# Second-stage tokens in the weight landing buffers, and two output-weight loads in flight

## The chip, the cores and the metric

The kernel runs on one core of a Trainium2 chip. What counts is the device time of one execution, in microseconds: the median over the runs of a kernel. Beside it stands one profiled execution, with the span from its first to its last instruction and a trace of every engine. The engines are TensorE (PE), VectorE (DVE), ScalarE (ACT), GpSimd (POOL) and SyncE (SP). In this kernel SP issues all the transfers between memory and the core's own memory (SBUF), one after the other, from one queue.

## The reference

Block-causal attention over 4 batches of 8 heads (576 tokens, 64 wide), then a first feed-forward block with three input matrices, then a second one with a gate. All values are float32.

```python
scores = np.where(mask, scale * np.matmul(q, k.transpose(0, 1, 3, 2)), -1e9)
attn = softmax(scores)                                # block 64, causal
x = heads_merged(np.matmul(attn, v))                  # 2304 x 512
h = np.maximum(np.maximum(x @ w1, x @ w2), x @ w3)    # 768 wide
x = h @ w_out                                         # moe: 2304 x 512
gate = 1.0 / (1.0 + np.exp(-(x @ w_gate)))            # 1536 wide
out = gate * (x @ w_val) @ w_out                      # moe2: 2304 x 512
```

## The kernel before, in words

Every float32 operand is split into a rounded high part and the rest (`fp32r`), and each product is three matmuls: high by high, high by low, low by high (L535 to L537, L574 to L576, L1220 to L1222).

**First stage** (attention and the first block), TensorE 0 to 475.5 us. Attention heads come in pairs (`job`), the first block in token groups (`gates`, `outs`): groups 0 to 3 are the early 256 tokens of each batch, 4 to 7 the late 320. A gate block of a group is three groups of twelve matmuls (`experts`) into two PSUM banks `ps_m`; ACT copies the first result to `m`, DVE takes two maxima (`larger`, L545), ACT and DVE split the maximum into `HR` (`high_h`, L558, and `low_h`). Six blocks are followed by four column blocks of the projection (`project`), whose results leave through `x2s` (L97 or L93) to `x2d` in memory (`store`, L595, three stores for each column block of a late group). The last group, 7, has its six gate blocks from 433.2 to about 465 and its projection until 475.5. While the first stage runs, the second stage's weights are also *parked*: each 64-bit weight piece is loaded (`take`, `praw`), shifted (L759), prepared on ACT (L755) and joined to float32 words (L770), and stored to memory again. `park_pair` does this for 24 pieces of the gate and value weights, and writes the seven combinations (`pairs`) that a seven-product block multiplication needs; `park_out` does it for the 12 pieces of the output weights (`outw` to `outs`). All of it uses the pool `raw` of four buffers of 4 KB: a piece takes one for its load and one for its joined words.

The order of each engine in the first stage comes from a planner in the kernel (`plan`). An `Op` has an engine, a cost, what it depends on, and for parking an earliest time: piece n of the pairs stands at `park0 + park * n`, piece f of the output weights `parko * f` after the last pair. The list `order_` holds what the next load has to wait for. The planned order is written out as it stands, and each engine then works it off in sequence.

**Second stage**, TensorE from 475.5 us. Tokens come in three chunks of 768. `take_x` loads a chunk (`xraw`, 1.5 MB), forms four differences with DVE (`t`, pool `tt`, L1116) and splits four blocks and the three kept combinations into `xc0` to `xc6` (ACT L1120 and DVE L102): eighteen instructions. `after_group` only keeps each of them behind a given conversion of group 7 on its engine. `take_w` loads parts x, z, y of an expert's weights (`wr`, four buffers), splits them on ACT (L1159) and on DVE or POOL (L102), and stores the low part for later chunks (`lowp`, L1166). TensorE runs seven products of six matmuls for each of the twelve experts: for the first one the products 0, 5, 4, 1, 6, then for each further one 0, 5, 4, 3 of the expert before, 1, 2 of the expert before, 6. Then the output projection of the chunk follows. DVE, ACT, POOL and SP are ordered here by a scheduler from the written times.

The second stage's pools are allocated one after the other from the bottom of SBUF, over the first stage's closed ones. Which first-stage tile lies under a second-stage tile decides what its first writer waits for. From the bottom, the first stage has `XT` (the attention's output, 26 KB, read by the gate matmuls), the four `raw` buffers, `tmp` (the `m`), `x2s`, eight weight tiles `w`, `HR`, and then the attention's own tiles. In the kernel before, `xr`, `ost`, `hid0` and the first bytes of `wr` lie on `XT`, the rest of `wr` and the first `pt` on `raw`, and `tt` on the end of `HR`.

Of the kernel before, what the change touches and what calls it, by code (L numbers as in the profile page):

```python
# [61 lines left out]
    "load": 14.95,  # L62
    "park0": 112,
    "park": 18.3,
    "parko": 8.0,
    "slack": 100.0,
    "spare": 0.17,
    "start": 53.02,
# [10 lines left out]
def block_attention_moe_moe(ctx: ExitStack, tc, kq1, v1, kq2, vt, wa, wb, out):  # L79
# [5 lines left out]
    def f32(ap):  # L85
        return ap.bitcast(F32)
# [38 lines left out]
    def load(out, src):  # L125
        nc.sync.dma_start(out=out.bitcast(U64) if wide else f32(out), in_=src)
# [39 lines left out]
    def act(n, acc=0):  # L166
        return ("A", 0.19 + 0.00073 * n + 0.2 * acc)
# [481 lines left out]
    t, vn = P["t0"], 0  # L649

    def visit(t):
        for j, s in visits[vn]:
            place[j.i, s] = t
            t += LEN[s][int(j.late)]
        return t

    while vn <= ends[0]:
        t = visit(t) + P["gap0"]
# [12 lines left out]
    for k, (mm, upto) in enumerate(stretches):  # L671
        n_v = ends[upto] + 1 - vn if upto < 2 * B else 0
        v0 = vn
        for n, (i, f, w) in enumerate(mm):
# [4 lines left out]
            while vn < v0 + n_v and (vn - v0 + 1) * (len(mm) - P["tail" if k > 3 else "tail1"] * (k > 0)) <= (n + 1) * n_v:  # L679
                t = visit(t)  # L680
# [3 lines left out]
    def build():  # L684
# [57 lines left out]
        def word_ops(i, t, ring, dest, dring=None):  # L742
            box = {}

            def take():
                box["x"] = raw_p.tile([128, PC * (1 + wide)], U32, tag="raw", name="praw")
                load(box["x"], wb[i])

            def words():
                w = box["x"].rearrange("p (n w) -> p n w", w=2)  # L750
                return w[:, :, 0], w[:, :, 1], w[:, :, 1].bitcast(F32)

            def first_part():
                x = words()[2]
                A.activation(x, x, AF.Prelu, scale=2.0 ** -112, alpha=2.0 ** 32)  # L755

            def shift():
                lo = words()[0]
                V.tensor_scalar(out=lo, in0=lo, scalar1=29, scalar2=None, op0=ALU.logical_shift_right)  # L759

            def two(x):
                return x.rearrange("p (a n) -> p a n", a=2)

            def join():
                o = dest()
                if not wide:
                    V.tensor_copy(o, two(f32(box["x"])))
                    return
                lo, hi, _ = words()
                V.scalar_tensor_tensor(  # L770
                    out=o.bitcast(U32), in0=two(hi), scalar=3, in1=two(lo),
                    op0=ALU.logical_shift_left, op1=ALU.bitwise_or,
                )

            ld = Op("S", 0.1, take, ring, ring="raw", size=512e3)
            new, deps = [ld], [ld]
            if wide:
                p = Op(*act(PC), first_part, [ld])
                s = Op("V", 0.36, shift, [ld])
                deps = [p, s]  # L780
                new += deps
            j = Op("V", 0.72, join, deps, ring=dring)
            new.append(j)
            for o in new:
                o.early, o.late = t, t + P["slack"]
            ld.early = t - P["load"]
            ld.frees = [j]
            return ld, j

        def put(out, src, deps, t):  # L790
            d = Op("S", 0.1, lambda: nc.sync.dma_start(out=out, in_=src()), deps, size=512e3)
            d.early, d.late = t, t + P["slack"]
            return d

        order_ = []
# [47 lines left out]
        def park_out(f):  # L843
            t = P["park0"] + P["park"] * NF2 + P["parko"] * f
            box = {}

            def dest():
                box["d"] = raw_p.tile([128, PC], F32, tag="raw", name="outw")
                return box["d"].rearrange("p (a n) -> p a n", a=2)

            ld, j = word_ops(3 * f + 2, t, list(order_), dest, "raw")
            order_[:] = [j]
            j.frees = [put(outs_d[f], lambda: box["d"], [j], t)]

        never = Op("V", 0.0, lambda: None, [])
# [206 lines left out]
    def pool(name, bufs, **kw):  # L1062
        return ctx.enter_context(tc.tile_pool(name=name, bufs=bufs, reuse_waits="tile", **kw))
# [4 lines left out]
    def hidden(n):  # L1068
        p = pool(f"hid{len(HID)}", 1)
        HID.extend(p.tile([128, 2, HC], F32R, name=f"hid{len(HID) + k}") for k in range(n))  # L1070
# [3 lines left out]
    def combos(ks):  # L1074
        p = pool(f"xc{len(XC)}", 1)
        for k in ks:
            XC[k] = p.tile([128, 2, 2, N2], F32R, name=f"xc{k}")

    xr_p = pool("xr", 1)
    ost_p = pool("ost", 3)  # L1080
    hidden(1)
    wr_p = pool("wr", 4)
    pt_p = pool("pt", 17)
    wg_p = pool("wg", 2)
    ow_p = pool("ow", 4)
    hidden(11)
    tt_p = pool("tt", 2)
    combos((0, 4, 5, 1, 6, 3, 2))
    warm = pool("warm", 1).tile([128, 8], F32, name="warm")
    acc_p = pool("acc", 8, space=PSUM)  # L1090
    PD, OU = 6 * 0.1735, 3 * 0.2317
# [195 lines left out]
    t = TB  # L1287
# [10 lines left out]
    for c in range(TOK // HC):  # L1298
# [11 lines left out]
        def second(n, t):  # L1310
            on(t, product(c, n, 1, "a", False))
            t += PD
            finish(c, n, 0, 0, None, t + 0.01)
            return t
# [27 lines left out]
        for n in range(NF2):  # L1342
            t = first(n, t)
            if n:
                t = fourth(n - 1, t)
            t = second(n, t)
            if n:
                t = third(n - 1, t)
            t = seventh(n, t)
            if 6 <= n < 10:  # L1350
                take_o(c, n - 6, t + 1.5)
        for f in range(NF2):
            for i in range(6):
                if f == 0 and i == 3:
                    t = third(NF2 - 1, fourth(NF2 - 1, t))
# [70 lines left out]
```

## Time and profile before

| what | us |
|---|---|
| median of 3 runs | 903.88 (903.22 to 905.01) |
| profiled execution, its own time | 905.0 |
| its span, first to last instruction | 903.1 |
| TensorE busy | 874.9 (97%), mean granted clock 0.992 |
| DVE, ACT, POOL busy | 587.3, 447.0, 97.2 |
| chain that ended last | PE 91%, DMA 4%, DVE 3%, SP's queue 1% |

The page divides the span into 40 slices of 22.6 us. TensorE's busy share is 9 tenths or more in nearly all; lower are the first two, one in the middle of the span, and the last. The page's list of groups gives for each line and engine the busy time, the mean duration of one instruction, and the idle time ahead of it with what ended it. The granted clock is shown as a share of the full 2.4 GHz. In a timeline row the first number is the start, the second the duration, and the bracket the idle time of that engine just before the instruction and what released it.

### The profile page before, as it was taken

How to read it: one execution, taken by the hardware profiler on the slowest of the kernel's cores; microseconds unless marked ns; L12 is line 12 of the kernel's file. 1: busy time of each engine (PE TensorE's matmuls, PEld its weight loads, DVE VectorE, ACT ScalarE, POOL GpSimd, SP SyncE). 2: the span in 40 equal slices, each digit the busy share in tenths (PEclk: the TensorE clock that was granted, in tenths of full speed). 3: DMA queues.
4: the chain of work that ended last, by engine and by line, in shares of the span. 5: the costliest groups of instructions: out<-in, count | busy, mean ns of one | idle time of the engine just before them, and what ended most of it. 6: DMA issues, size and time to landing. Idle time of an engine off the chain costs nothing.

```text
span 903.1 us, 15107 instructions
## 1 busy us (share of the span) xinstructions
PE 874.9 (97%) x5432; PEld 794.6 (88%) x5432; DVE 587.3 (65%) x1367; ACT 447.0 (49%) x1014; POOL 97.2 (11%) x91
## 2 busy tenths in 40 slices
PE   5899999999999999999996999999999999999997
PEld 4788889887989898899995999988999988999986
DVE  7999859996789699685338788731555621555400
ACT  7897547562554364353224555622666622666311
POOL 0000000000000000000003444300232300222300
PEclk9999999999999999999997999999999999999999
DMA  9921244445534534423446779854789853788232
GB/s 341 371 82 36 86 166 146 145 138 184 180 102 150 185 103 140 131 76 120 155 171 212 267 242 310 313 158 135 249 257 307 302 150 123 246 261 298 87 105 81
DMA packets 82810, 165.09 MB, mean 183 GB/s; under 512 B 10800, under 2 KB 23600, under 8 KB 82736
## 3 DMA queue, kind: packets, MB, share of 16 engines
q1 hardware_dynamic: 82736, 164.14, 54.8%
q8 instruction: 42, 0.69, 0.3%
q14 instruction: 32, 0.26, 0.1%
HBM read 126.35 MB, written 37.75 MB: 182 GB/s over the span
## 4 chain that ended last, share of the span: by engine, by line
PE 91%; DMA 4%; DVE 3%; SPq 1%; issue 0%; ACT 0%; DVEq 0%; ACTq 0%
PE acc L1220 10%; PE acc L1222 10%; PE acc L1221 10%; PE ps_m L535 8%; PE ps_m L537 8%; PE ps_m L536 8%; PE acc L1276 5%; PE acc L1275 5%; PE acc L1274 5%; PE ps_o L488 5%; PE ps_t L452 4%; PE ps_s L376 3%; PE ps_m L574 2%; PE ps_m L576 2%; PE ps_m L575 2%; DMA qk<-in_kq_dram 2%
## 5 line engine op out<-in xcount | busy, mean ns | idle before, releaser
L535 PE MATMUL ps_m<-XT,w 128*128 128x320 f32 (+2 forms) x504 | 163.7, 325 | 2.7 <-DVE x2s L97 2.7
L537 PE MATMUL ps_m<-XT,w 128*128 128x320 f32 (+2 forms) x504 | 158.0, 313 | 0.2 <-DVE w L102 0.2
L536 PE MATMUL ps_m<-XT,w 128*128 128x320 f32 (+2 forms) x504 | 157.9, 313 | 0.0
L535 PEld LDWEIGHTS ps_m<-XT,w 128*128 128x128 f32 x504 | 95.1, 189 | 10.5 <-issue 3.5
L537 PEld LDWEIGHTS ps_m<-XT,w 128*128 128x128 f32 x504 | 95.0, 188 | 3.4 <-DVE w L102 0.5
L536 PEld LDWEIGHTS ps_m<-XT,w 128*128 128x128 f32 x504 | 95.2, 189 | 2.7 <-DVE XT L102 0.2
L400 ACT ACTIVATE E<-ps_s,nm 128x256 f32<-128x256 f32 (+3 forms) x128 | 66.3, 526 | 40.5 <-PE ps_t L452 33.1
L1275 PE MATMUL acc<-ow,hid 128*128 128x512 f32 x216 | 84.2, 390 | 0.0
L1276 PE MATMUL acc<-ow,hid 128*128 128x512 f32 x216 | 84.2, 390 | 0.0
L1274 PE MATMUL acc<-ow,hid 128*128 128x512 f32 x216 | 84.1, 389 | 0.0
L1220 PE MATMUL acc<-xc,wgx 128*128 128x384 f32 x216 | 73.5, 340 | 3.5 <-ACT xc L1120 3.5
L1222 PE MATMUL acc<-xc,wgx 128*128 128x384 f32 x216 | 73.1, 338 | 1.3 <-POOL wgx L102 1.3
L1221 PE MATMUL acc<-xc,wgx 128*128 128x384 f32 x216 | 73.2, 339 | 0.8 <-DVE xc L102 0.8
L97 DVE COPY osb<-acc 128x512 f32<-128x512 f32 x6 | 4.2, 692 | 95.5 <-PE acc L1276 88.5
L545 DVE TENSOR_TENSOR m<-ps_m,m 128x320 f32<-128x320 f32 (+2 forms) x84 | 41.7, 496 | 29.0 <-PE ps_m L537 28.4
L1188 ACT CAST ow<-or 128x512 fp32r<-128x512 f32 x36 | 22.3, 621 | 73.4 <-PE acc L1276 55.4
L1233 DVE TENSOR_TENSOR u<-acc,p 128x384 f32<-128x384 f32 x72 | 39.9, 554 | 26.6 <-PE acc L1222 19.6
L395 DVE TENSOR_REDUCE nm<-ps_s 128x1 f32<-128x256 f32 (+3 forms) x128 | 55.0, 472 | 2.2 <-ACT E L400 2.2
L102 POOL TENSOR_TENSOR wgx<-wr,wgx 128x768 fp32r<-128x768 f32 x1 | 1.8, 1810 | 474.2 <-DMA x2d<-x2s 474.2
L1233 DVE TENSOR_TENSOR u<-acc,u 128x384 f32<-128x384 f32 x72 | 40.1, 557 | 18.1 <-PE acc L1222 16.8
L452 PE MATMUL ps_t<-ident,E 128*128 128x128 f32 x320 | 44.9, 278 | 6.2 <-DVE E L99 4.3
L1220 PE MATMUL acc<-xc,wgz 128*128 128x384 f32 x144 | 48.8, 339 | 1.9 <-DVE u L1233 1.1
(122 smaller groups left out, 2092.9 us busy)
## 6 DMA issues: line engine op xcount, KB each, us to landing
praw<-in_wb_dram SPq DMA_DIRECT2D x36, 512.0 KB, 4.3
wr<-pairs SPq DMA_DIRECT2D x72, 256.0 KB, 3.5
wr<-pairs SPq DMA_DIRECT2D x36, 384.0 KB, 4.3
or<-outs SPq DMA_DIRECT2D x36, 256.0 KB, 3.7
wgx<-lowp SPq DMA_DIRECT2D x24, 384.0 KB, 3.7
wland<-in_wa_dram SPq DMA_DIRECT2D x5, 1536.0 KB, 16.1
qk<-in_kq_dram SPq DMA_DIRECT2D x16, 480.0 KB, 3.4
wgz<-lowp SPq DMA_DIRECT2D x24, 256.0 KB, 4.2
```

The lines of the kernel that those rows point to most:

```text
L400: A.activation(E[h][:, e : e + 128 * (t + 1)], j.s[h, t], AF.Exp, bias=j.nm[:, c : c + 1], scale=1.0, accum_out=j.sm[:, c : c + 1],)
L452: T.transpose(ps[:, 128 * i : 128 * i + 128], E[h][:, e : e + 128], ident)
L535: T.matmul(ps, wt[:, 0, w, k], xh[:, k], start=(k == 0), stop=False)
L536: T.matmul(ps, wt[:, 0, w, k], xl[:, k], start=False, stop=False)
L537: T.matmul(ps, wt[:, 1, w, k], xh[:, k], start=False, stop=(k == KD - 1))
L1220: T.matmul(ps, w[:, 0, h], x[:, 0, h], start=start and h == 0, stop=False, skip_group_check=True)
L1221: T.matmul(ps, w[:, 0, h], x[:, 1, h], start=False, stop=False, skip_group_check=True)
L1222: T.matmul(ps, w[:, 1, h], x[:, 0, h], start=False, stop=h == 1, skip_group_check=True)
L1233: V.tensor_tensor(out=o, in0=BK[c, n, b][:, :N2], in1=x, op=ALU.add)
L1274: T.matmul(ps, h[:, 0, ct], w[:, 0], start=(f == 0), stop=False)
L1275: T.matmul(ps, h[:, 0, ct], w[:, 1], start=False, stop=False)
L1276: T.matmul(ps, h[:, 1, ct], w[:, 0], start=False, stop=(f == NF2 - 1))
```

## The change

Two things are changed. The parking of output weights is planned every 4 us instead of every 8, and a load waits for the piece two before it (`order_[:1]` of a list of two) instead of the piece before it. And the second stage's pools are allocated in another order: `wr` and two `hid` tiles come to lie on `XT`, `ost` on the first `raw` buffer, `xr` exactly on the other three, the `pt` tiles on `tmp`, `x2s` and the first weight tiles, `xc6` on a weight tile, and `tt` with the remaining `xc` tiles on the attention's memory behind `HR`. No instruction is added or removed.

```diff
-    "parko": 8.0,
+    "parko": 4.0,
...
-            ld, j = word_ops(3 * f + 2, t, list(order_), dest, "raw")
-            order_[:] = [j]
+            ld, j = word_ops(3 * f + 2, t, order_[:1], dest, "raw")
+            order_[:] = order_[-1:] + [j]
...
+    wr_p = pool("wr", 4)
+    hidden(2)
+    ost_p = pool("ost", 3)
     xr_p = pool("xr", 1)
-    ost_p = pool("ost", 3)
-    hidden(1)
-    wr_p = pool("wr", 4)
     pt_p = pool("pt", 17)
     wg_p = pool("wg", 2)
+    combos((6,))
     ow_p = pool("ow", 4)
-    hidden(11)
+    hidden(10)
     tt_p = pool("tt", 2)
-    combos((0, 4, 5, 1, 6, 3, 2))
+    combos((0, 4, 5, 1, 3, 2))
```

TensorE's order stays as it was. On SP, before, the end of the parking, the load of the tokens and the first weight loads follow one another (`praw` a parking load, `outs` a parking store, `wr` the weights' raw parts):

```order
L791 DMA outs_95<-outw 128x512
L126 DMA praw<-in_wb_dram 128x512
L791 DMA outs_96<-outw 128x512
L1106 DMA xraw<-x2d 128x4x768
L1155 DMA wr<-pairs_73 128x768
L1155 DMA wr<-pairs_73 128x512 x2
```

After the change, right behind the last parking store, SP has this (the first three stores are the first column block of group 6's projection):

```order
L595 DMA x2d<-x2s 128x128
L595 DMA x2d<-x2s 128x64
L595 DMA x2d<-x2s 128x128
L1107 DMA xraw<-x2d 128x4x768
L595 DMA x2d<-x2s 128x128
L595 DMA x2d<-x2s 128x64
L595 DMA x2d<-x2s 128x128 x2
L595 DMA x2d<-x2s 128x64
L595 DMA x2d<-x2s 128x128 x2
L595 DMA x2d<-x2s 128x64
L595 DMA x2d<-x2s 128x128
L1156 DMA wr<-pairs_73 128x768
```

The token load has moved ahead of the rest of group 6's stores, and so ahead of all of group 7's gate blocks. On DVE, before, two gate blocks of group 7 (`m` the maxima, `HR` the low part) have parking work between them:

```order
L545 TENSOR_TENSOR m_5556<-ps_m,m_5536 128x320
L545 TENSOR_TENSOR m_5571<-ps_m,m_5556 128x320
L102 TENSOR_TENSOR HR<-m_5571,HR 128x320
L759 TENSOR_SCALAR praw<-praw 128x512
L770 SCALAR_TENSOR_TENSOR outw<-praw 128x512
L545 TENSOR_TENSOR m_5607<-ps_m,m_5588 128x320
L545 TENSOR_TENSOR m_5625<-ps_m,m_5607 128x320
```

After the change the same place has the tokens' differences and low parts (`t` a difference, `xc_5926` to `xc_5928` low parts of token blocks):

```order
L102 TENSOR_TENSOR HR<-m_5590,HR 128x320
L102 TENSOR_TENSOR xc_5926<-t_5943,xc_5926 128x768
L1117 TENSOR_TENSOR t_5955<-xraw,t_5943 128x768
L545 TENSOR_TENSOR m_5622<-ps_m,m_5607 128x320
L545 TENSOR_TENSOR m_5637<-ps_m,m_5622 128x320
L102 TENSOR_TENSOR HR<-m_5637,HR 128x320
L102 TENSOR_TENSOR xc_5927<-t_5955,xc_5927 128x768
L102 TENSOR_TENSOR xc_5928<-xraw,xc_5928 128x768
L1117 TENSOR_TENSOR t_5969<-xraw,t_5955 128x768
L545 TENSOR_TENSOR m_5669<-ps_m,m_5654 128x320
```

Of the eighteen token instructions only the two of `xc6` still stand behind group 7 on their engines. In the attention, on DVE before, one parked piece stands between a softmax's scaling (`E_151`) and the split of the attention's output (`XT`), at 380.7 us of the trace:

```order
L545 TENSOR_TENSOR m_4854<-ps_m,m_4837 128x320
L99 TENSOR_SCALAR E_151<-E_151,rc 128x512
L759 TENSOR_SCALAR praw<-praw 128x512
L770 SCALAR_TENSOR_TENSOR outw<-praw 128x512
L97 CAST XT<-ps_o 128x320
L102 TENSOR_TENSOR XT<-ps_o,XT 128x320
```

After the change there are two, and the high part of `XT` is ACT's:

```order
L545 TENSOR_TENSOR m_4863<-ps_m,m_4846 128x320
L99 TENSOR_SCALAR E_151<-E_151,rc 128x512
L759 TENSOR_SCALAR praw<-praw 128x512 x2
L770 SCALAR_TENSOR_TENSOR outw<-praw 128x512 x2
L102 TENSOR_TENSOR XT<-ps_o,XT 128x320
```

The other pieces of the second half have moved in the same way, to between 381 and 425 us of the trace, the last of them ahead of the first `x2s` copy of group 6.

## Rows read from the trace of the kernel before

**Rows 1.** TensorE's waits, 475 to 496 us: us in total, times, longest.
```profile
PE acc L1220 <- ACT xc L1120: 3.5, 1, 3.5
PE acc L1222 <- POOL wgx L102: 1.3, 1, 1.3
PE acc L1220 <- DVE u L1233: 1.1, 1, 1.1
PE acc L1220 <- ACT p L1304: 0.8, 1, 0.8
PE acc L1221 <- DVE xc L102: 0.8, 1, 0.8
```

**Rows 2.** Windows: length; PE, PEld, DVE, ACT, POOL busy; clock, DMA, GB/s.
```profile
475.50:495.98 20.48, 12.95 (x49) 11.27 (x49) 17.25 (x18) 9.14 (x15) 7.05 (x4) 0.75 0.66 201
495.98:516.46 20.48, 20.48 (x120) 20.48 (x120) 15.97 (x25) 12.28 (x23) 9.21 (x8) 1.00 0.81 273
```

**Rows 3.** SP's queue around the border, timeline: start, us, what.
```profile
460.88 0.32 SPq L791 DMA_DIRECT2D outs<-outw  x1
465.04 0.54 SPq L1106 DMA_DIRECT2D xraw<-x2d  x1
...
482.86 4.11 SPq L595 DMA_DIRECT2D x2d<-x2s  x5
```

**Rows 4.** DMA issues (pairs' parking; its end; the border): KB, median us to landing.
```profile
praw<-in_wb_dram SPq DMA_DIRECT2D x23, 512.0 KB, 4.7
...
praw<-in_wb_dram SPq DMA_DIRECT2D x5, 512.0 KB, 3.5
outs<-outw SPq DMA_DIRECT2D x6, 256.0 KB, 2.1
...
xraw<-x2d SPq DMA_DIRECT2D x1, 1536.0 KB, 7.3
```

**Rows 5.** Timeline of DVE and POOL at the border.
```profile
475.60 2.57 DVE L1116 TENSOR_TENSOR t<-xraw 128x768 f32<-128x768 f32 x1 [0.41 <-PE ps_m L576]
...
485.60 0.94 DVE L1116 TENSOR_TENSOR t<-xraw 128x768 f32<-128x768 f32 x1
...
475.55 1.81 POOL L102 TENSOR_TENSOR wgx<-wr,wgx 128x768 fp32r<-128x768 f32 x1 [474.24 <-DMA x2d<-x2s]
```

**Rows 6.** Timeline of DVE, then ACT, 365 to 436 us.
```profile
369.22 0.43 DVE L759 TENSOR_SCALAR praw<-praw 128x512 uint32<-128x512 uint32 x1 [5.02 <-DMA praw<-in_wb_dram]
...
400.81 0.49 DVE L545 TENSOR_TENSOR m<-ps_m,m 128x320 f32<-128x320 f32 x1 [1.09 <-PE ps_m L537]
...
411.10 0.49 DVE L97 CAST XT<-ps_o 128x320 fp32r<-128x320 f32 x1 [1.24 <-PE ps_o L488]
...
425.44 0.49 DVE L97 COPY x2s<-ps_m 128x320 f32<-128x320 f32 x1 [1.80 <-PE ps_m L576]
...
435.12 0.43 ACT L543 COPY m<-ps_m 128x320 f32<-128x320 f32 x1 [0.87 <-PE ps_m L537]
```

**Rows 7.** Timeline of DVE, first maximum of a late gate block of group 7.
```profile
458.07 0.49 DVE L545 TENSOR_TENSOR m<-ps_m,m 128x320 f32<-128x320 f32 x1 [2.08 <-PE ps_m L537]
```

**Rows 8.** Tile `wr`, 460 to 540 us: ns min/median/max; last, us to landing.
```profile
L1159 ACT CAST wgx<-wr x9: 826/836/838, 474.6 to 532.6; 128x768 fp32r<-128x768 f32 x9
L1159 ACT CAST wgz<-wr x9: 604/616/622, 475.4 to 537.1; 128x512 fp32r<-128x512 f32 x9
L102 POOL TENSOR_TENSOR wgz<-wr,wgz x9: 1292/1609/2005, 477.3 to 538.6; 128x512 fp32r<-128x512 f32 x9
...
L102 DVE TENSOR_TENSOR wgx<-wr,wgx x8: 946/958/1144, 487.3 to 533.5; 128x768 fp32r<-128x768 f32 x8
...
DMA to landing us min/median/max: 2.7/4.1/8.8
```

**Rows 9.** Window in the attention, columns as in rows 2.
```profile
380.00:390.00 10.00, 10.00 (x82) 8.84 (x79) 9.59 (x27) 3.75 (x10) 0.00 (x0) 1.00 0.37 113
```

**Rows 10.** TensorE's waits, 330 to 476 us: us in total, times, longest.
```profile
PE ps_m L535 <- DVE x2s L97: 1.7, 1, 1.7
```

## Prediction, made before the change was run

> **What bounds the kernel now.** I read the page first: TensorE is busy for 97% of the span and makes up 91% of the chain that ended last, so only a moment in which it stands still, or runs at its lower clock, can be won. The windows along the span then show where it stands: at the head, at the tail, and at the border between the two stages. The list of its waits in that border stretch [rows 1] has five entries, 3.5 + 1.3 + 1.1 + 0.8 + 0.8 = 7.5 us, and all five name work on the second stage's first tokens or first weights. The two windows of equal length [rows 2] say what the border costs in all: 475.50 to 495.98 holds 48 of the second stage's matmuls (the 49th of the row is the first stage's last, in flight at the edge), the next 20.48 us hold 118 starts (the row counts 120, two of them cut by the edges). So one matmul needs 20.48/118 = 0.1735 us, 48 need 8.3 us, and the border wastes 20.48 - 8.33 = **12.15 us**: 7.5 us of waits, and 4.6 us because after the gaps the granted clock is 0.75 on the mean (part of it at the 1.2 GHz level) and the array refills.
>
> Next I asked why the tokens are late. The queue on SP [rows 3] stores the last parked output weight at 460.88 and issues the load of `xraw` only at 465.04: its place in memory is that of `XT`, which the last gate matmul reads until then. The load takes 7.3 us [rows 4], and DVE starts the first difference `t` at 475.60 [rows 5], released by the last projection matmul, as `tt` lies on `HR`. Everything behind it, eighteen conversions on two engines, runs while TensorE waits.
>
> **The change part by part.** *The tokens' place.* `xraw` now covers three of the four `raw` buffers, whose last user is the parking, and `tt` lies in the attention's memory, free since about 425. In the new order of SP the load stands behind the stores of the last-but-one projection's first column block, that is at 425.44 [rows 6] plus the copy and three stores: about 427.3, instead of 465.04. It took 7.3 us with four weight loads queued behind it, so it lands by 434.6. Nothing is added; the eighteen conversions move.
>
> *Where they move to.* In the new order of DVE two or three of them stand between the `HR` subtraction of one gate block and the first maximum of the next. In the trace DVE is idle there for 2.08 us in the blocks without parking work [rows 7], and parking work is gone from all of them. Two pieces of 0.94 us (the quiet `t` row [rows 5]) make 1.9 us, which fits; three make 2.8 us, 0.8 too many, and the second maximum has room of about 1.2 us to take it up. So I cost them at nothing; if that cover were gone, 0.8 us twice. The duration is a choice: the same instruction took 2.57 us at 475.60 and 0.94 at 485.60 [rows 5], and the first ran while GpSimd worked (its row starts at 475.55). I take 0.94, since GpSimd has no instruction before the border in the new order either. The Trainium skill, page "SBUF — State Buffer", section "Who interferes with whom", says a VectorE instruction with two SBUF inputs is held off entirely by a GpSimd instruction that reads SBUF; the trace agrees (2.57 against 0.94). By it alone the sum stays: the moved pieces would leave GpSimd's company.
>
> *What is left at the border.* The four `wr` buffers now lie in `XT`, so the first weight loads are issued at 465.04, no longer behind 1.5 MB of tokens. With the median landing of 4.1 us the first is in at 469.1, ACT casts 0.84 us, GpSimd's longest conversion takes 2.0 us [rows 8]: 472, before TensorE comes at 475.5. With the worst landing, 8.8, it is 476.7, about 1 us late. Of the tokens only `xc6` is left: DVE runs the last `x2s` copy (0.49 [rows 6]), `wgy` (two thirds of a `wgx`, some 0.7), `xc6` and `wgx` (0.95 each [rows 5, 8]), 3.1 us from 475.6, then `u` (384 columns where a maximum of 320 takes 0.49 [rows 7], so some 0.6) to 479.3. TensorE's fifth product, which needs it, would start at 475.5 + 4 x 1.04 = 479.7. So the first five products run through.
>
> *The second pair of weights* loses its lead, and here I see a price. Part z of the second expert is loaded after the last three token stores: 476.1 + 3 x 0.82 (five took 4.11 [rows 3]) = 478.6 at the worst, 0.4 for the store ahead, so issued by 479.0; 4.1 to land, 0.62 on ACT, 1.3 to 2.0 on GpSimd [rows 8]: 485.0 to 485.7. TensorE wants it after nine products and two matmuls, 475.5 + 9 x 1.04 + 0.35 = 485.2. Part x of the third is issued 2 us later, 481.0, lands at 485.1, 1.8 us for both conversions: 486.9, some queueing on ACT, wanted at 475.5 + 12 x 1.04 + 0.35 = 488.3. Bounds: no stall with the quickest landing (2.7), some 3.5 us with the slowest (8.8). I take **0.5 us**, near the median. After that each load is a whole expert (7.3 us) ahead, as in the trace, and TensorE is full until the tail.
>
> *The parking.* Twelve pieces, each a load of 512 KB, a shift (0.43 [rows 6]) and a join on DVE and a store: none is added, but all twelve now end before 425.44 instead of 460.88, so five or six more of them, some 1.1 us of DVE each by the 512 columns, meet the attention, where DVE is busy 9.59 of 10 us [rows 9] in the worst stretch. The new order puts one more pair there at 381 and takes a copy of 0.49 to ACT in exchange (+0.6), one at 400 and one at 409, where DVE was idle for 1.09 and 1.24 us [rows 6]. From 330 to 476 TensorE waits for another engine once [rows 10], so the lag of a few tenths has to use up a lead first. The first piece keeps what it has: DVE stood until 369.22 for its load [rows 6], with an `x2s` copy behind it, and that copy is the one wait, 1.7 us, of [rows 10]. Bounds: a gain of that 1.7 if the load comes sooner, a loss of 5.5 us (five pieces in full) if nothing hides them. I take **0.3 us** lost, nearest to the rows with idle time. Two loads in flight landed in 4.7 us while pairs were parked, one alone in 3.5 [rows 4]; with 4.7 the pieces that the new order has at 412 and 415.5 come 0.5 to 1 us late, beside the 1.24 us of idle DVE. The Trainium skill, page "DMA: Bandwidth & Descriptors", section "Issuing engines are not separate DMA queues", says all transfers run on the same 16 engines and interleave; by it the second load buys start-up time only, not bandwidth, and that speaks for the 4.7. The sum would not move.
>
> *ACT's new wait.* The warm-up of the sigmoid now stands ahead of the last stretch's first `m` copy and waits for `xraw` (434.6). That copy ran at 435.12 [rows 6], and TensorE needs its bank a gate group (twelve matmuls of 320 columns, 1.7 us) later: hidden, unless the load lands after 436.5.
>
> **The sum**, against the profiled execution (905.0 us, span 903.1, so 1.9 around it): -12.15 + 0.5 + 0.3 = -11.35, 893.7. That execution lies 1.1 above the median of the three runs, 903.88, so the forecast for the median is **892.5 us**.
>
> **The rivals.** *Weights come late* (the border's wait is replaced by another): landing took up to 8.8 us [rows 8]; then z and x of the next experts stall TensorE by 3 to 4 us, and half-clock matmuls after the gap add up to 2: 895.5 to 898.5. For it: the lead of the second pair is near nothing. Against: few bytes move at 476 to 481.
> *Parking crowds the attention*: DVE lags at 381 to 425 and a few evictions or transposes come late, 1 to 4 us: 893.5 to 896.5. Against it is the idle time at 400 to 425.
> *Slower than before*: the `raw` ring has four buffers and each piece takes two, one for the load and one for the joined words. If the second load must wait until the store before has landed, a piece takes 3.5 to 4.7 + 1.1 + 0.4 + 2.1 = 7.1 to 8.3 us [rows 4]; twelve from 364.5 end at 450 or later, while DVE's order puts the last one ahead of the `x2s` copy of 425.44 [rows 6]. TensorE would stand some 25 us: about 917. It decides from 1.4 us of delay for each of the last eight pieces (11.35/8). Against: in the new order each load waits for a store at least two stores back.
> *It does not do what it says*: `xraw` still lands near the border because the parking drags, without holding TensorE: 903.9. Against it stands its row in SP's order.
>
> **How the numbers follow.** Forecast 0.70 (890.5 to 894.2), late weights 0.13, crowding 0.10, no change 0.03, slower 0.04. The range 890.0 to 897.5 takes in the forecast with its bounds, crowding, and the lower half of late weights, and leaves out about 0.15. A measurement of this kernel tells about 0.2% from no change: faster 0.93, within 0.03, slower 0.04.
>
> **What would show it.** `xraw` issued near 427 and landed near 434; DVE's `t` rows between 440 and 462, at about 0.95 us; TensorE's second-stage matmuls 0.17 us apart from 475.6 on, no granted clock under 1.0 there; the next 20 us free of waits over 1 us. Wrong would be: a TensorE wait on `wgz` or `wgx` of several us at 485 to 490, a wait on DVE or ACT between 371 and 437, or loads of `praw` issued only after the store just before them has landed.

## The result, and the profile after

The changed kernel takes **895.9 us** (median; 895.0 to 896.7) against 903.56 us for the kernel before beside it: a ratio of 0.9912, 95% interval 0.9895 to 0.9929. Three more comparisons, told of below, gave 0.9899, 0.9911 and 0.9895, that is 894.5, 896.3 and 894.5 us. So the change gains 7.7 to 9.7 us, about 1%. The forecast was 892.5 with a range of 890.0 to 897.5: the direction is right and the time lies in the range, but the gain was put 1.7 to 3.7 us too high. This part is about where these went.

First the border. These are the same two windows as [rows 2], then the list of TensorE's waits that answers to [rows 10], of the kernel after. Columns of the first: window; its length; PE, PEld, DVE, ACT, POOL busy with their instructions; granted clock, DMA share, GB/s.

```profile
475.50:495.98 20.48, 20.48 (x120) 20.48 (x120) 12.95 (x22) 9.98 (x19) 6.56 (x5) 1.00 0.87 288
495.98:516.46 20.48, 20.11 (x115) 19.47 (x114) 15.87 (x26) 11.82 (x24) 10.59 (x9) 1.00 0.89 295
```

```profile
PE ps_m L535 <- DVE x2s L97: 1.8, 1, 1.8
```

In the first window TensorE was busy for 12.95 us and now is for all 20.48, with 120 matmuls where there were 49, and the granted clock is 1.00 (the 2.4 GHz level) where it was 0.75 on the mean. The list of waits between 475 and 496 us that held the five entries of [rows 1] is empty. The second window has turned the other way: 20.48 us busy before, 20.11 now, and the DMA share stands at 0.89.

SP's queue and DVE's timeline show why the border is clean (start, length, engine, line, operation, tiles; in brackets the idle time before it):

```profile
427.76 0.54 SPq L1107 DMA_DIRECT2D xraw<-x2d  x1
...
465.40 1.74 SPq L1156 DMA_DIRECT2D wr<-pairs  x4
```

```profile
440.43 0.95 DVE L1117 TENSOR_TENSOR t<-xraw 128x768 f32<-128x768 f32 x1
...
446.58 0.95 DVE L1117 TENSOR_TENSOR t<-xraw,t 128x768 f32<-128x768 f32 x1
...
452.73 0.95 DVE L1117 TENSOR_TENSOR t<-xraw,t 128x768 f32<-128x768 f32 x1
453.60 0.48 DVE L545 TENSOR_TENSOR m<-ps_m,m 128x320 f32<-128x320 f32 x1
454.84 0.49 DVE L545 TENSOR_TENSOR m<-ps_m,m 128x320 f32<-128x320 f32 x1 [0.76 <-PE ps_m L537]
```

The load of `xraw` is issued at 427.8 and not at 465.04 [rows 3], lands in 7.3 us, and the differences are made from 440 on, between the gate blocks, at 0.95 us each. Where three pieces stand in a row (450.99 to 453.60) the first maximum is some 0.45 us late (by the blocks' step of 5.28 us it would stand at 453.15), and the idle time ahead of the second falls to 0.76 from 1.20; TensorE does not wait.

Both traces hold the same 5432 matmuls in the same order, so their starts can be set side by side one by one. Four stretches come out (the last projection matmul is the 3272nd; us; the four columns on the right are profiles of the changed kernel, the last three from the experiments):

| stretch | before | after | again | beside | third |
|---|---|---|---|---|---|
| start to the last projection matmul | 475.3 | 475.6 | 475.2 | 475.4 | 476.1 |
| from there over 49 starts (the border) | 20.73 | 8.47 | 8.47 | 8.47 | 8.47 |
| the next 430 (nearly all the rest of the first chunk's pairs) | 75.77 | 77.55 | 76.75 | 80.21 | 78.15 |
| the last 1681 | 326.25 | 326.25 | 326.25 | 326.25 | 326.25 |

The border gives 12.26 us against the one profile of the kernel before, in every profile of the changed kernel. The stretch behind it costs 1.0 to 4.4 us more than before, 2.4 on the mean, and another amount in each execution. These are TensorE's waits there (484 to 600 us), of the first profile, then of the one called "beside":

```profile
PE acc L1221 <- DVE u L1234: 1.7, 3, 1.2
```

```profile
PE acc L1221 <- ACT wgz L1160: 1.8, 1, 1.8
PE acc L1221 <- DVE u L1234: 1.7, 3, 1.2
PE acc L1223 <- DVE wgx L102: 0.2, 1, 0.2
```

All the entries on `u` are one kind: the fourth product of an expert (its weights are `wgy`) needs a PSUM bank that DVE's addition `u` must have read. The longest of them, at 545.20, is not new: the same matmul waits 0.9 us for `u` in the kernel before, at 555.33.

### The profile page after: what moved, and what is told of

Its sections match the earlier page's. It is cut to its first block, busy times and chain, and to the rows that moved or that the text cites. A ratio compares the mean times of both kernels' runs of the same rounds, so it can differ in the third digit from the quotient of the medians.

```text
span 892.9 us, 15107 instructions
## 1 busy us (share of the span) xinstructions
PE 870.0 (97%) x5432; PEld 789.6 (88%) x5432; DVE 582.0 (65%) x1367; ACT 446.0 (50%) x1014; POOL 96.4 (11%) x91
## 4 chain that ended last, share of the span: by engine, by line
PE 85%; DMA 7%; DVE 3%; SPq 2%; issue 1%; ACT 1%; POOL 1%; ACTq 0%; POOLq 0%; DVEq 0%
PE ps_m L535 9%; PE ps_m L537 8%; PE ps_m L536 8%; PE acc L1221 7%; PE acc L1222 7%; PE acc L1223 7%; PE acc L1276 5%; PE acc L1277 5%; PE acc L1275 5%; PE ps_o L488 5%; PE ps_t L452 4%; PE ps_s L376 3%; PE ps_m L574 2%; PE ps_m L576 2%; PE ps_m L575 2%; DMA qk<-in_kq_dram 2%
## 5 line engine op out<-in xcount | busy, mean ns | idle before, releaser
L1223 PE MATMUL acc<-xc,wgx 128*128 128x384 f32 x216 | 72.2, 334 | 0.0
L1221 PE MATMUL acc<-xc,wgx 128*128 128x384 f32 x216 | 72.2, 334 | 0.0
L1222 PE MATMUL acc<-xc,wgx 128*128 128x384 f32 x216 | 72.2, 334 | 0.0
L1221 PE MATMUL acc<-xc,wgy 128*128 128x384 f32 x144 | 48.6, 337 | 1.8 <-DVE u L1234 1.7
```

What stands on the lines that cost most here:

```text
L1221: T.matmul(ps, w[:, 0, h], x[:, 0, h], start=start and h == 0, stop=False, skip_group_check=True)
L1222: T.matmul(ps, w[:, 0, h], x[:, 1, h], start=False, stop=False, skip_group_check=True)
L1223: T.matmul(ps, w[:, 1, h], x[:, 0, h], start=False, stop=h == 1, skip_group_check=True)
```

## The experiments

**The same kernel again.**

> The changed kernel a second time, so that the size of its gain does not hang on two profiled executions. By medians it gained 7.7 us (895.9 against 903.56), by the two profiled executions 10.1, while matmul for matmul the border alone gave 12.1. Theory (border 12.1 gained, about 1.7 given back in the first chunk by VectorE's late u additions, the rest is which execution was profiled): 894.5 to 896.5 beside a median of before of 903 to 904, and in the profile the four late products again, 1 to 2.5 us in all. Rival (something that varies between executions takes 2 us at the border or in the attention): the profile of this run shows the border's gain under 11 us, or TensorE waits before 475 us of over 1 us that the first profile did not have.

Measured: 894.53 us against 903.78, ratio 0.9899 (0.9885 to 0.9912). The border is 8.47 us to the hundredth, and TensorE waits for `u` twice, 1.4 us in all. The theory holds; between these two profiles the part before 475 us differs by less than half a microsecond.

**The places in memory alone.** The new pools, and the parking as before, one load in flight:

```diff
-    "parko": 4.0,
+    "parko": 8.0,
...
-            ld, j = word_ops(3 * f + 2, t, order_[:1], dest, "raw")
-            order_[:] = order_[-1:] + [j]
+            ld, j = word_ops(3 * f + 2, t, list(order_), dest, "raw")
+            order_[:] = [j]
```

> The new places in memory alone; the parking keeps one load in flight. The raw buffers that xraw now lies on are then free only when the last parked store, issued at 460.9, has landed: xraw issued at about 463, landed at 470, instead of 434. Theory (the parking is what brings the tokens early, and the tokens' conversions are the border): the first t starts at 470 to 471, thirteen pieces of VectorE at 0.5 to 0.95 us end near 484, the fifth product, wanted at 479.7, waits some 4 us, and the clock falls with it: 897 to 900, half of the gain. Rival (the new places do it all, the parking is not needed): 895 to 896.5, no TensorE wait over 1 us between 475 and 496. Rival (VectorE, waiting for the tokens, holds back the last projection copies, which stand behind t in its order): TensorE waits on x2s before 476 and 900 or more.

Measured: 902.15 us, ratio 0.9988 (0.9977 to 0.9999). The border takes 18.0 us, a gain of 2.7 where the whole change gains 12.3. The first theory forecast half of the gain and a wait at the fifth product; it failed. The third possibility is what happened, a little later than it said. TensorE's waits of this kernel from 475 to 500 us, then DVE's timeline:

```profile
PE acc L1221 <- DVE x2s L97: 6.9, 1, 6.9
```

```profile
466.87 0.96 DVE L1117 TENSOR_TENSOR t<-xraw 128x768 f32<-128x768 f32 x1
...
473.75 2.57 DVE L1117 TENSOR_TENSOR t<-xraw,t 128x768 f32<-128x768 f32 x1
476.24 2.02 DVE L102 TENSOR_TENSOR xc<-xraw,xc 128x768 fp32r<-128x768 f32 x1
478.19 0.94 DVE L1117 TENSOR_TENSOR t<-xraw 128x768 f32<-128x768 f32 x1
479.06 0.68 DVE L102 TENSOR_TENSOR wgy<-wr,wgy 128x512 fp32r<-128x512 f32 x1
479.66 0.95 DVE L102 TENSOR_TENSOR xc<-t,xc 128x768 fp32r<-128x768 f32 x1
480.52 0.48 DVE L97 COPY x2s<-ps_m 128x320 f32<-128x320 f32 x1
```

The tokens are in at 466.9, since `xraw` is issued at 460.05, right behind the last parked store. Behind the copy at 469.00, ten pieces (nine of the tokens and a `wgy`) stand ahead of the next copy `x2s` of the last projection, which runs at 480.52. The second stage's first product accumulates into the bank that this copy empties, and waits 6.9 us for it. A token conversion that comes too late is not only late itself: on an in-order engine it holds back what stands behind it. The number `parko` by itself changes nothing: the program built with 4 is the one built with 8, with one load in flight as with two. The second load in flight is the whole of the parking's edit.

**The parking alone.** The old pools with the new parking:

```diff
-    wr_p = pool("wr", 4)
-    hidden(2)
-    ost_p = pool("ost", 3)
     xr_p = pool("xr", 1)
+    ost_p = pool("ost", 3)
+    hidden(1)
+    wr_p = pool("wr", 4)
...
-    combos((6,))
     ow_p = pool("ow", 4)
-    hidden(10)
+    hidden(11)
     tt_p = pool("tt", 2)
-    combos((0, 4, 5, 1, 3, 2))
+    combos((0, 4, 5, 1, 6, 3, 2))
```

> The two loads in flight alone, with the old places in memory. Theory (all of the gain is at the border, and there the old places hold xraw to 465.04 whatever the parking does): 903.2 to 904.3 beside 903.6, the last parked store near 424, xraw issued at 465 as before. Rival (the earlier parking crowds the attention and takes back part of the gain): 904.5 to 906.5, with TensorE waits on DVE or ACT between 365 and 437 that before does not have. Rival (parking out of the border's way is itself worth something): 900 to 902.

Measured: 904.85 us, by the median a little over the theory's range; the ratio to the runs of before at its side is 1.0007 (0.9997 to 1.0017), no change. SP's queue, TensorE's waits from 330 to 475 us, and those from 475 to 500 us:

```profile
420.67 2.75 SPq L791 DMA_DIRECT2D outs<-outw  x2
...
463.66 0.54 SPq L1106 DMA_DIRECT2D xraw<-x2d  x1
```

```profile
PE ps_m L535 <- DVE x2s L97: 0.6, 1, 0.6
PE ps_m L535 <- ACT m L543: 0.4, 1, 0.4
```

```profile
PE acc L1220 <- ACT xc L1120: 3.5, 1, 3.5
PE acc L1222 <- POOL wgx L102: 1.1, 1, 1.1
PE acc L1221 <- DVE xc L102: 1.0, 1, 1.0
PE acc L1220 <- ACT p L1304: 0.6, 1, 0.6
```

The last stores leave 40 us earlier. The load of `xraw` leaves 1.4 us earlier (463.66 for 465.04), and by 1.4 us this whole execution is ahead at the last projection matmul (473.9 for 475.3): it still waits for `XT`. The waits are those of [rows 1], nearly entry by entry. The attention carries the earlier pieces with 1.0 us of waits where [rows 10] has 1.7. So the parking alone shows neither cost nor gain, to within the interval; it frees the place that the tokens need. The border takes 19.9 us here with the same work in it as before, where the profile of before has 20.73: the border itself seems to vary between executions, by what one profile of each can tell.

**The differences left on `HR`.** The changed kernel, `tt` moved back:

```diff
-    hidden(10)
+    hidden(6)
     tt_p = pool("tt", 2)
+    hidden(4)
```

> The changed kernel, but with the differences' buffers tt left on HR, so that the raw tokens are early and the differences are not. Theory (half of the border is the four differences and the conversions that hang on them): t starts again at 475.6, xc6, the eleventh piece of VectorE from there, is ready near 485, the fifth product waits some 5 us for it and the second one 2, and the clock drops after them: 900 to 903.5. Rival (the early tokens alone do it, VectorE catches up under the first products): 896 to 898.

Measured: 900.2 us, ratio 0.9961 (0.9947 to 0.9975), within the theory's range. The second product waits 2.1 us as it said, and then 1.0 more; the wait for the fifth is 2.2 us and not 5. The border takes 16.59 us, 8.1 more than with `tt` in the attention's memory. TensorE's waits from 475 to 500 us, and DVE's first difference:

```profile
PE acc L1222 <- ACT p L1306: 2.2, 1, 2.2
PE acc L1222 <- ACT xc L1122: 2.1, 1, 2.1
PE acc L1223 <- DVE xc L102: 1.0, 1, 1.0
...
```

```profile
475.25 0.96 DVE L1118 TENSOR_TENSOR t<-xraw 128x768 f32<-128x768 f32 x1 [2.15 <-PE ps_m L576]
```

So early raw tokens and weights give 4 us of the border's 12, the early differences the other 8. The first `t` takes 0.96 us at the same point of the program at which it took 2.57 [rows 5]: here GpSimd has its first two conversions behind it, there it was at work.

**Four kernels on the loss behind the border.** They were run together with the changed kernel.

> The changed kernel once more, on the chip of the three variants of it that follow, so that differences of 1 us between them can be read: 894 to 896, TensorE's late products (the one that needs u from VectorE) at four or fewer places between 500 and 550, 1.5 to 2.5 us in all.

Measured: 896.31 us against 904.39, ratio 0.9911 (0.9893 to 0.9928). The profiled execution gave back 4.4 us, not 1.5 to 2.5, and one wait is of another kind. ScalarE's timeline at it, then TensorE's:

```profile
497.84 0.83 ACT L1160 CAST wgx<-wr 128x768 fp32r<-128x768 f32 x1 [4.59 <-DMA wr<-pairs]
```

```profile
498.65 0.34 PE L1223 MATMUL acc<-xc,wgx 128*128 128x384 f32 x1
500.75 0.41 PE L1221 MATMUL acc<-xc,wgy 128*128 128x384 f32 x1 [1.75 <-ACT wgz L1160]
```

A weight load landed late, ScalarE stood 4.6 us for it, DVE's low part of the same weights came at 498.71, and `u` stood behind that and ended at 500.60. TensorE started again at 500.75. The profile names the cast of `wgz`, which ended at almost the same moment (500.62); by what the product reads, `u` is the nearer cause. Either way the delay began with the load.

The first variant gives TensorE one product more between the bank's two uses:

```diff
             t = first(n, t)
+            t = second(n, t)
             if n:
                 t = fourth(n - 1, t)
-            t = second(n, t)
```

> The changed kernel with one edit in TensorE's order: of each expert the second product stands ahead of the fourth product of the expert before, so that VectorE has four products of 1.04 us instead of three between the seventh product and the fourth, whose bank its addition u must read first. Theory (what the changed kernel gives back between 500 and 550 is u, late by 0.2 to 1.3 us behind wgy and behind GpSimd's work): those waits go or fall under 0.4 us in all, 892 to 893.5, some 1.5 to 2 us under the changed kernel. Rival (the weights as a whole come late, their loads and stores fill the DMA engines to 87% there): the wait moves to wgz or wgx, the time stays at 894 to 896 or rises, since part z is wanted two products sooner.

Measured: 895.18 us, ratio 0.9904 (0.9888 to 0.9920). The waits on `u` are gone, but others have taken their place (TensorE's list, 475 to 600 us):

```profile
PE acc L1221 <- ACT p L1305: 2.0, 3, 1.3
```

The time and the stretch of 77.73 us are what the changed kernel itself takes, as the rival said, though the waits went to `p` and not to `wgz` or `wgx`. So more room for `u` wins nothing back: the place at which the loss shows moves.

The second does without the first chunk's stores of low parts:

```diff
         if c == 0:
             on(t + 0.7, rest)
-            on(t + 2.0, keep)
...
-            nc.sync.dma_start(out=f32(WG[c, n, part][:, 1]), in_=lowp_d[n][:, k0:k1])
+            nc.sync.dma_start(out=f32(WG[c, n, part][:, 1]), in_=pairs_d[n][:, k0:k1])
```

> The changed kernel without the stores of the low parts of the pair weights in the first chunk; the later chunks read as many bytes from the high-precision pair weights in their place, so their low parts are not what they should be. It takes 10.5 MB of stores from the stretch in which time is given back. Theory (u is late because VectorE's additions stand behind wgy and are slowed beside GpSimd, not because of the DMA): the waits on u stay within half of what they were, 893.5 to 895.5. Rival (the DMA engines, at 87% there, bring the weights late and push VectorE's conversions onto the additions): the waits go, 892 to 893.3.

Measured: 893.45 us, ratio 0.9879 (0.9864 to 0.9893), at the edge between the two expectations by the time, and the rival's by the profile. TensorE's waits from 484 to 600 us, then the window 496 to 560 us of this kernel and of the changed one:

```profile
PE acc L1220 <- DVE u L1233: 0.7, 1, 0.7
```

```profile
496.00:560.00 64.00, 63.35 (x364) 62.74 (x364) 51.99 (x83) 39.01 (x75) 31.05 (x26) 1.00 0.60 179
```

```profile
496.00:560.00 64.00, 62.17 (x354) 60.87 (x353) 51.70 (x82) 37.90 (x74) 30.31 (x26) 1.00 0.89 290
```

With the DMA share at 0.60 for 0.89 the stretch takes 76.0 us for 77.55 to 80.21, and of two to five waits one of 0.7 us is left, with DVE, ACT and GpSimd as busy as they were. So what is given back hangs on the stores.

The third takes the low part of `hid` from GpSimd to DVE in the first chunk:

```diff
-            on(t + 1.1, lambda: sub("G", HID[f][:, 1, ct], SG[c, p, fi, j], f32(HID[f][:, 0, ct])))
+            on(t + 1.1, lambda: sub("V" if c == 0 else "G", HID[f][:, 1, ct], SG[c, p, fi, j], f32(HID[f][:, 0, ct])))
```

> The changed kernel, but in the first chunk the low part of hid is made on VectorE and not on GpSimd, two pieces of about 0.5 us an expert more on VectorE and two of 1.0 to 1.3 us less on GpSimd. Theory (the 1.37 us of an addition of 0.56 us, at 527.3 and 543.3, comes from GpSimd working beside it on hid): the additions that were 1.37 are 0.56, but VectorE is busy some 6.5 of 7.3 us an expert, so the sum is open: 893 to 896. Rival (VectorE's length has nothing to do with GpSimd): additions of 1.37 remain at the same places, and with 1 us more of work an expert the waits grow: 896 to 900.

Measured: 897.62 us, ratio 0.9936 (0.9913 to 0.9959), over the theory's range and in the rival's. DVE's slow piece, and GpSimd beside it:

```profile
527.07 1.64 DVE L1251 TENSOR_TENSOR u<-u,u 128x384 f32<-128x384 f32 x1
```

```profile
526.76 1.53 POOL L102 TENSOR_TENSOR wgz<-wr,wgz 128x512 fp32r<-128x512 f32 x1 [5.78 <-DMA wr<-pairs]
```

The addition is still slow, now beside `wgz` instead of `hid`. The rival's reason does not hold all the same: between 470 and 600 us of this profile the eleven additions of this kind (L1251) with no GpSimd work beside them take 0.55 to 0.56 us. GpSimd's company lengthens it, beside `wgz` as beside `hid`; taking away one of two tiles only moves the meeting, and DVE's extra work made the waits longer (3.0 us on `u`).

**Three ways with the stores.** Again with the changed kernel beside them.

> The changed kernel beside three variants that treat the low-part stores of the first chunk in other ways. Its profiles so far differ by 2.4 us in the first chunk alone (a weight load that landed late held ScalarE for 4.6 us in the second one). Theory now (the weight loads have little lead once TensorE no longer stands at the border, and a late landing costs what the lead can't hide): 893.5 to 897.5, with ScalarE waiting several us for weight loads between 480 and 550.

Measured: 894.45 us against 904.14, ratio 0.9895 (0.9878 to 0.9912), with 2.2 us of waits on `u` in the profile, and 7.2 us in which ScalarE waits for weight loads between 484 and 560 us.

```diff
+        first = 1 if n < 6 else 0
...
-        if c == 0:
+        if c <= first:
             on(t + 0.7, rest)
-            on(t + 2.0, keep)
+            if c == first:
+                on(t + 2.0, keep)
```

With `n < 12` in place of `n < 6` it holds for all twelve.

> The changed kernel, but the low parts of all twelve pair weights are stored in the second chunk, which makes them a second time, instead of in the first. The first chunk is then as in the run without these stores (893.45), at the price of VectorE's and GpSimd's conversions in the second chunk, where the stores and loads together are as many bytes as before. Theory (lead is lost only where TensorE follows the border without a pause; the second chunk starts with the weights far ahead): 892.5 to 894.5, under the changed kernel by 1.5 to 3 us. Rival (the late u additions and the slow pieces beside GpSimd cost the same in whichever chunk they stand): 895 to 898, waits on u near 700 to 790.

> The same for the first six pair weights only. Theory (the lead is built while the first six stream in without their stores, and then holds): 892.5 to 894.5, as with all twelve, with half of the second chunk's conversions. Rival (stores cost wherever they meet loads and the first chunk's conversions): the waits on u at 529 and 545 stay, 894.5 to 896.

Measured: 893.37 us, ratio 0.9885 (0.9867 to 0.9903), and 893.44 us, ratio 0.9884 (0.9869 to 0.9898). TensorE's waits from 475 to 860 us, of the first and of the second:

```profile
PE acc L1223 <- DVE u L1236: 0.5, 2, 0.3
PE acc L1223 <- ACT p L1307: 0.2, 1, 0.2
```

```profile
PE acc L1223 <- DVE u L1236: 1.1, 1, 1.1
```

The stretch takes 75.77 and 76.66 us; the second chunk pays 1.3 us with twelve and 0.2 with six (327.55 and 326.43 for 326.25). The profiles say what the theory said. Both times lie 1 us under the changed kernel's, but the intervals overlap, so that these two are better than it is likely and not shown. Against the kernel before they are 1.2% faster.

```diff
-            nc.sync.dma_start(out=lowp_d[n][:, k0:k1], in_=f32(WG[c, n, part][:, 1]))
+            nc.scalar.dma_start(out=lowp_d[n][:, k0:k1], in_=f32(WG[c, n, part][:, 1]))
```

> The changed kernel with the low-part stores issued from ScalarE's queue and not from SP's, the bytes the same. It tells whether the stores cost by their bytes (DMA engines 86% busy) or by their place in SP's order, where a weight load stands behind a store that waits for VectorE. Theory (bytes): landing of weight loads as before (median 4.2, up to 6 or 7 us), ScalarE 0.1 to 0.3 us more a store and some waits for VectorE: 895 to 899. Rival (SP's order): loads issued earlier, ScalarE's waits for weight loads under 3 us in all, 892.5 to 894.5.

Measured: 903.14 us, ratio 0.9987 (0.9976 to 0.9999), worse than either expectation. ScalarE's timeline (ACTq is its queue):

```profile
473.11 0.34 ACTq L1167 DMA_DIRECT2D lowp<-wgx  x1
475.92 0.35 ACTq L1167 DMA_DIRECT2D lowp<-wgz  x1
478.36 0.35 ACTq L1167 DMA_DIRECT2D lowp<-wgy  x1
478.75 0.83 ACT L1121 CAST xc<-t 128x768 fp32r<-128x768 f32 x1 [8.20 <-DMA x2d<-x2s]
```

ScalarE waits, in order, for the low parts that it is to store; the cast of `xc6`, which the changed kernel makes at 471, comes at 478.75, and TensorE stands 3.8 us at the border. Weight loads came sooner (ScalarE waits 1.6 us for them from 484 to 560), but ScalarE was late itself, and a TensorE that stands at the border gives the loads their lead again, so this run cannot tell whether the stores cost by their bytes or by their place in SP's order. That stays open. The Trainium skill, page "DMA: Bandwidth & Descriptors", section "Issuing engines are not separate DMA queues", says that issuing from another engine saves only the time of the issue; no run here can check that saving. This trace shows a price beside it, the wait of the engine that issues: ScalarE idle for 8.20 us ahead of its cast.

One row of every profile sums this up, ScalarE's wait for the pair weights between 484 and 560 us: 4.1 us before, 6.7 to 8.3 in the four profiles of the changed kernel, 1.4 to 1.7 where the first stores are left out or put off. Of before, of after, and with six put off:

```profile
ACT wgx L1159 <- DMA wr<-pairs: 2.7, 1, 2.7
ACT wgz L1159 <- DMA wr<-pairs: 1.4, 1, 1.4
```

```profile
ACT wgx L1160 <- DMA wr<-pairs: 4.8, 4, 1.5
ACT wgy L1160 <- DMA wr<-pairs: 2.6, 2, 1.3
```

```profile
ACT wgx L1160 <- DMA wr<-pairs: 1.4, 2, 1.3
```

## Why the prediction was right, and where it was not

The main term, the border, came out as worked out. The time lies in the range, but not where the forecast had put itself, at 890.5 to 894.2: 895.9 falls into the part that the range took in for the rivals.

*The border* (-12.15): measured 20.73 to 8.47, 12.26 us. The way of reading it held: two windows of the same length, and the count of matmuls in the one times the pace of the other. It catches what the list of waits (7.5 us) misses. Of the other 4.6 us, 3.1 are twenty starts that lie 0.32 to 0.49 us apart instead of 0.17, from 483.4 to 486.7 and from 490.3 to 493.6, in stretches where the granted clock is 0.50, the 1.2 GHz level (479.8 to 486.6 and 490.1 to 493.4); that the array refills, no run shows. The two marks set for it, `xraw` issued near 427 and `t` at about 0.95 us from 440 on, came out within a microsecond. Taking 0.95 and not 2.57 for `t` was right, though not for the reason given: GpSimd does work before the border in the new order, but from 469.45 on, behind the last `t` at 458.01.

*The second pair of weights* (+0.5): hardly paid, and with nothing to spare. In the first profile part z was issued at 478.3 (forecast: by 479.0) and part x of the third expert at 481.2 (forecast 481.0), and TensorE has no wait before 500 us. But the low part of x was ready at 488.25 and not at 486.9, at the moment it was wanted; in the profile "beside" it came too late, and TensorE waited 0.2 us for it. The upper bound of 3.5 us fits part x only; by the same rows part z with the slowest landing comes to 4.5 or more.

*The parking* (+0.3): nothing that can be told from the spread. The starts up to the last projection matmul differ by -0.1 to +0.8 us, and the parking alone is no change. Where crowding was feared it cost nothing: the last 671 starts up to that matmul (from about 381 us on) take 93.71 us in every profile of every kernel here, the kernel before included. What varies lies ahead of them. The rival that the second load would have to wait for the store before it, some 25 us, did not come about.

*Behind the border* (0): **this step failed.** It said that after the second pair "each load is a whole expert (7.3 us) ahead, as in the trace, and TensorE is full until the tail". That was read from the trace of before, in which TensorE had stood 12 us at the border while the weights ran ahead. The change takes away that pause and with it the lead. The traces show it directly. These are the low part of part x of the third expert's weights, as DVE makes it, and TensorE's first matmul on these weights, before and after:

```profile
491.37 0.96 DVE L102 TENSOR_TENSOR wgx<-wr,wgx 128x768 fp32r<-128x768 f32 x1 [1.15 <-ACT wgx L1159]
500.15 0.33 PE L1220 MATMUL acc<-xc,wgx 128*128 128x384 f32 x1
```

```profile
487.29 0.96 DVE L102 TENSOR_TENSOR wgx<-wr,wgx 128x768 fp32r<-128x768 f32 x1 [1.03 <-ACT wgx L1160]
488.25 0.33 PE L1221 MATMUL acc<-xc,wgx 128*128 128x384 f32 x1
```

The lead was 7.8 us and is nothing; for the next expert it was 9.1 and is 3.3, and only the ninth has as much as before. Without the stores the two are 3.2 and 8.1. And where TensorE still stands at the border, with all the stores in place (the places alone, the parking alone, `tt` on `HR`), the first is 5.3 to 7.4 us, and the 430 starts take 75.7 to 76.0, as before. So it takes both for the loss: no pause at the border, and the stores beside the loads.

The DMA share from 496 to 560 us is 0.89, where the kernel before has 0.82 in the same window, and a load that lands late now reaches TensorE through ScalarE's cast, DVE's low part and the `u` behind it. Cost: 1.0 to 4.4 us, 2.4 on the mean. The rival "weights come late" had the mechanism, but at 485 to 490 us, as a stall of 3 to 4 us in one place; it came as two to five waits of 0.2 to 1.8 us between 488 and 548. That it needs the stores is shown by the run without them; whether they act by bytes or by order is not. How a load that is not late for TensorE can hold it up shows at 506.4 us of the first profile: ScalarE stands 1.25 us for the sixth expert's `wgx` and casts it at 501.37, DVE makes its low part at 502.24 (7.5 us before TensorE reads it), and the `u` that stands behind it on DVE, wanted for the fourth expert, ends at 506.32. What causes the smaller waits at 514 and 529 us is not shown.

*From the profiled execution to the median* (-1.1): too much to take off the changed kernel as well. The span from the first to the last instruction has a median of 901.9 us over 49 runs of the kernel before and of 893.1 over 20 of the changed one, so the profiled execution of before, with 903.1, lay 1.2 over its median, while 903.1 less the 9.9 below is the changed kernel's median span without any more taken off. The parking alone has 0.8 us less at a border with the same work, so part of the 1.1 lay, it seems, in what the change removes, and was counted twice (one execution of each, so this is argued and not shown).

With the terms as measured: 12.26 - 2.4, and no other term that shows, is 9.9 us against the profiled execution, or 895.1; that is where the four medians lie (894.5 to 896.3), without the 1.1.

*What each part does*: the places alone gain 0.1%, the parking alone nothing, both together 1%. The prediction treated the parking as a cost that the change must bear, and did not ask what the places would be worth without it.

## What to carry to other kernels

A stall gives a lead to every stream that goes on during it. When a change removes the stall, read the next stretch anew: who waits for loads there, at which DMA share, and how much of the lead was only the stall. And where one edit frees a place for another, price them as a pair: here either alone is worth next to nothing. An in-order engine that is given work whose data may come late also delays what stands behind that work; look there first, not at the late work itself.

## What the runs showed of the hardware

A DVE addition of 0.55 us took 1.37 beside GpSimd's work on `hid` and 1.64 beside `wgz`; a `t` of 0.95 took 2.57. The Trainium skill, page "SBUF — State Buffer", section "Who interferes with whom", says that a VectorE instruction with two inputs in SBUF contends with a GpSimd instruction that reads SBUF; these rows agree, and GpSimd's own rows grow too (`wgz` 1.28 to 1.75 us). Which of the two grows goes, in these rows, by which started first, so "held off entirely" in the prediction is one half of it. In the changed kernel the addition at 527.29 came behind a GpSimd row of 526.93 and took 1.37; the one at 511.53 came 0.12 us ahead of one, kept its 0.56, and GpSimd's row took 1.32 where it takes 1.01 alone.

The median landing of a weight load was 3.1 us from 475 to 550 us without the stores, and 3.9 to 4.3 in the four profiles with them (3.8 in the kernel before); the slowest took 4.8, and 5.4 to 7.2 (5.7). The changed kernel spreads between executions from 892.6 to 898.6 us, and the kernel before as widely, from 901.7 to 907.4, though the last 1681 matmuls take the same 326.25 us each time. In the four profiles the stretch behind the border varies by 3.5 us, the rest by 0.9 at most. Part of the spread lies outside the span: a time exceeds its span by 1.9 to 5.0 us.
